# Two interleaved transformer layers on one core: small prices in the planner, and TensorE's order written anew

## The chip, the cores and the metric

The kernel runs on one core of a Trainium2 chip. The metric is the device time of one execution in microseconds (us); smaller is better. Below, TensorE is PE in the profile (its weight loads are PEld), VectorE is DVE, ScalarE is ACT, GpSimd is POOL, and SyncE, which issues most DMAs, is SP.

## The reference

Two layers of the same kind follow each other, with the same weights. Each is an attention over short segments that hands a small memory on from one segment to the next, and then a gated feed-forward network:

```python
for s in range(n_seg):                       # 64 segments of 32 rows
    h = concat([mem, xs])                    # 8 memory rows + 32 rows, 576 wide
    q, k, v = h @ Wq, h @ Wk, h @ Wv         # 32 heads of 128
    p = softmax(where(mask, q @ k.T * scale, -1e9))
    o = (p @ v) @ Wo
    mem = o[:, :M, :]                        # the next segment needs it
    outs.append(o[:, M:, :])
...
x = x + A(layernorm(x)); x = x + B(layernorm(x))   # B: (silu(x w1) * (x w3)) w2, 576 -> 4608 -> 576
x = x + A(layernorm(x)); x = x + B(layernorm(x))
```

The memory makes the segments of a layer a chain: segment s+1 can't start before segment s has its output.

## The kernel before

Both layers run at once, the second eight segments behind the first (`LAG`). There are 72 steps: in steps 0 to 7 the first layer alone is in work, in steps 8 to 63 both are, side by side in the columns of one operand (80 columns in place of 40), and in steps 64 to 71 the second alone. The feed-forward work of groups of four segments is filled in between.

`make_nodes` makes a list of some thousand pieces of work (`Node`), each with an engine, a price in us, the pieces that it depends on, and the buffers that it takes and frees (eight PSUM banks among them). Of TensorE's pieces, every kind has a letter (`KINDS`): `Q`/`q` the projections to queries and keys (576 = 4 x 128 + 64 contraction rows; the lower-case letter is the 64-row rest), `S` the scores of eight heads, `T` a transposition of the probabilities by matmul (in the steps with one layer; with two a DMA transposes them), `P` probabilities by values, `O`/`o` the output projection, `X x V v G g` the values, `F`/`f` the feed-forward's first matmuls, `W`/`w` its second, and `m a b p n` transpositions of rows.

The order of TensorE's pieces is written out as a string of letters, `ORDER = FIRST + FOUR * 11 + LAST`. FIRST has 773 letters, FOUR 208 (four steps; it is played eleven times), LAST 664. `plan` walks through the string and gives the pieces of the other engines, and the DMAs that SP issues, their places by playing the prices through: whichever engine has a piece that can start earliest takes it next. Pieces marked "AD" go to ACT or DVE, whichever comes first. So the string alone sets TensorE's order, and string and prices together set the order on DVE, ACT and on SP's queue, which issues in that order and waits where the next DMA is not yet allowed.

TensorE can use its array whole (`full`: 128 rows by 128 columns) or in parts that work side by side: `row` is two halves of 64 rows, `col` two halves of 64 columns, `c32`, `oct` and `quad` smaller parts of the value projections. Some pieces can run in one shape alone (`q` and `f` in row, `o` and the two-layer `S` in col, `Q` and `O` in full). Others can run in full or col ("full/col": `F`, `P`, `W`, `w`, `T`, `G` and the transpositions): in col every matmul of 128 output rows is issued as two of 64 (`mm`, lines 619 to 627). `plan` decides it by runs: a run of neighbours that can share a shape has that shape, and full where a run leaves the choice open. So a flexible piece next to an `o` or an `S` becomes col and saves a change of shape. A change is priced at `SWITCH = 0.098`.

All matmuls are recorded on line 627, all ACT work on line 630, DVE on 633, SP's loads on 636, the transposing DMAs on 1050. A transposing DMA (`ptd`) needs the probabilities from DVE, and `P` needs it landed. The weights of the feed-forward come in pieces by SP as their two buffers (`w13`) come free, which is when `F` and `f` of the piece two before are done.

At the very start, the first `Q` of step 0's units 0 and 4 (a unit is four heads) is preceded by 12 matmuls on the identity ("W,ident"), three on each quarter of the key weights as it lands; `qk` issues them only where the unit's `Q` comes ahead of its `q` (the name `first`).

Of the kernel before, what the change touches and what calls it, by code (L numbers as in the profile page):

```python
# [54 lines left out]

class Node:
    __slots__ = ("eng", "dur", "fn", "deps", "prio", "mode", "acq", "rel", "name", "lat", "outs", "left", "ready",
                 "start", "end", "by")

    def __init__(self, eng, dur, fn, deps=(), prio=0.0, mode=None, acq=(), rel=(), name="", lat=None):  # L60
# [3 lines left out]
        self.lat = lat  # L64
# [15 lines left out]
def plan(nodes, pools, letters):  # L80
# [119 lines left out]
def ewh(*ns):  # L200
# [2 lines left out]


FIRST = (
    "amQqQqqQqSTQQQqSqqqQSQSTXxVvPPTTOoPPOOooOoQQqqqqQSQQSqvVqQqqTSQPQOSToXPTOPTOPoxoOoQQqqqqQSQvVQSqqQqqQQSSTTPPOaOT"
    "oTPoPOOooQQqqqVvSQQqqQSQQqQqSTqPSxTXOPoTTOPPoOOooQqqpQQSQqqvVSnQqfFqqQQTSFqfTPQFOSfToPWOPfFTOPFOooofWQQqqqqQSQQS"
    "FFffqvVqqqQQQWTTSSFPffxXFPWOoTOPTFPOOoooffFQWQqqqqQQSFSfqVvfFQQqqWSQQFfqfTFSTPWPTOOoPofFTOPFOooWQqqfQQSQqqVvSFfQ"
    "qQqaWqqTQTPSQObSPoXXTTxxPOPOOoooQpqqqQQqSQvqnQfSFVfFqQQqfSFQPWqfSPFFOfOoPWoOofPFOoFfqqQQQQqqWSFSfqqQQqgqGSQQFPfg"
    "GWSfFPOGgfgFGoPOOPWOoooFFqfqfQQWSqqQQvFSqfVQQqqWSQFqfQfPaSFPOoOPoWOffFPFOooWQQqqqqQSQQbQqqSGSqgqQQPgGSOoPGggGPOO"  # L210
    "PooOoQqqqppQQQSvqqVnnQQSFqffFQQSqqfFSwPWPOOFffFooPwPOWOFooFqqffQQWQQwqqfFSFSqfqQwQQWGSqgqQFPfSGgggGPGOPoOOPwOWoo"
    "oFFqfqfQQQQqqfSWFVvwSFFqffqQQQQSqqWwPFSffPOOooFPwOWPFOooafQQqqWqSqqQQQQSqwbSQgqqQGSggGPGPOGPgoOPOOooo"
)
# [4 lines left out]
LAST = (  # L218
    "QqqqppQQQvSqVnSnqqQQQFSfqqQPFOSPofFOPwWOFPfooOofQQqqWwSFfqfFQQQQqfqqFWwGSSFffgqQFPGQWgqwOSoPFggfGGPOFPOOoooWwfqQ"
    "QQQvqqqVSSFqffQFQQQqqqwSWSPFPfOFOwWoPffFPOOoooWQQqqFSwfqfFQQqqWSQQQqqqQSVSbvVPwOPxvXoPOOPooOoQqqvppQVqqQSQQqqnnQ"  # L220
    "SFfqfqQQTSFSPTFPwOWTffoFPTOPOOoooWwFfqqfQQFSQvVqqqQQSQTWFqfqqQQSwSTPFffFOPwWoFTTffFPOPOOoowoXxvQQqqVqqQSQWSFqqfq"
    "QQQTSwqfQPFTSTOPWOFffoPTFOPWOooowVvfqqFQQQqqfSwQWSFFfqqqQQTWTSQPqPQOSwbOTXPxooTOPoOoQqqqpQQSQVqvQSqqQqnSQqTfQfPT"
    "SFPOOTFPooTOPwOfooFVvfqqQQFqqQSQFSwQqqfQQTSfqqFPQOTSXwPToxfOPTFPOOoooFfqqQQqqQSQQFSQfqqvVSwQQqqFTTSPPfFTOOfoPoTw"
    "POOooFfvVqqqQQwSQqQqfqQSFQQqqfSQTSTPPOOFToTPfPOOooopwfFFnFwffFFwffFFwwffFfFwFffFwFfFwffFFwffFfFwFfFwffFw"
)
ORDER = FIRST + FOUR * 11 + LAST

# [8 lines left out]
def make_nodes(em, nseg, pools, o=Opt, dma_bw=230e3, load_bw=400e3):  # L236
# [4 lines left out]
    def node(*a, **k):  # L241
        n = Node(*a, **k)
        nodes.append(n)
        return n
# [90 lines left out]
    def vg_nodes(t, g, deps, tail_deps):  # L335

        b = banks()
        for s in b:
            s.users = 2
        m_ = node("PE", 8 * 0.2158, em.vg(t, g, b, False), deps=deps, prio=t + o.vm, mode="full/col", acq=b, name="VG")  # L340
# [21 lines left out]
    def step(t):  # L362
# [18 lines left out]
        for g in range(NG):  # L381
            qs, qe = [], []
            for u in (2 * g, 2 * g + 1):
                q = Slot("qkt", users=1)
                b = banks()
                pq = t + o.qk + o.ustep * u
                m_ = node("PE", 32 * mm80, em.qk(t, u, b), deps=hx + hm[:1] + ([ld_h[u // 4]] if t == 0 else []),
                          prio=pq, mode="full", acq=[q] + b, name="QK")
                n = node("PE", 4 * mm80, em.qk_tail(t, u, b), deps=hx + hm + ([ld_h[u // 4]] if t == 0 else []), prio=pq + o.qkt, mode="row",
                         acq=[q] + b, name="QKt")  # L390
                rd += [m_, n]
                me[f"QK{u}"], me[f"QKt{u}"] = m_, n
# [22 lines left out]
                pts_of[t, g] = pe_[0]  # L415
            else:
                bt = banks(nl)
                tr = node("PE", 8 * (0.0258 if nl == 1 else 0.0358), em.ptr(t, g, pb, bt), deps=[pbs], prio=pf + o.tr, mode="full/col", acq=[pts] + bt, rel=[pb], name="TR", lat=0.265)
# [6 lines left out]
            b = banks()  # L425
            ot = Slot("ot")
            pv = node("PE", 8 * mm80, em.pv(t, g, pts, b), deps=pe_ + vx_ev["VM", t, g] + vx_ev["VX", t - e, g],
                      prio=pf + o.pv, mode="full/col", acq=b + [ot], rel=[pts], name="PV")
# [4 lines left out]
            wo = node("PE", 32 * mm80, em.wo(t, g, ot), deps=ote + ([ld_o[g]] if t == 0 else []), prio=t + o.wo + o.wog * g, mode="full",  # L433
                      acq=[y] if g == 0 else [], name="WO")
            wot = node("PE", 4 * mm80, em.wo_tail(t, g, ot), deps=[wo], prio=t + o.wo + o.wog * g, mode="col", rel=[ot], name="WOt")
            if g:
# [33 lines left out]
    def job(j):  # L470
# [36 lines left out]
        for at, pp in enumerate([npp - 1] + list(range(npp - 1)) if last else range(split, npp)):  # L507
# [5 lines left out]
            for pr_ in (2 * pp, 2 * pp + 1):  # L513
# [8 lines left out]
                else:  # L522
# [7 lines left out]
                htt = Slot("htt", users=ne)  # L530
                rel13 = [w13] if w13 else []
                fm = node("PE", 16 * mm, em.ffn_up(ents, pr_, w13, b, last and not stays, False), deps=wr + ld, prio=prio, mode="full/col",
                          acq=b + [htt], rel=rel13, name="FF")
# [7 lines left out]
            for (bi, g) in ents:  # L541
                b = banks()
                d = node("PE", 8 * 0.1225, em.ffn_down(em.col(bi, g), pp, htts, w2s, b, last and not stays), deps=mids + lds, prio=prio + o.w2,
                         mode="full/col", acq=b, rel=htts + w2s, name="W2b" if bi else "W2")
                if last and at == npp - 1:
                    xn = Slot("xn")
                    for h in (0, 1):
# [845 lines left out]
```

## Time and profile before

| what | us |
|---|---|
| three runs | 2629.52, 2633.95, 2636.86 (median 2633.95) |
| the profiled execution, whole | 2636.17 |
| its span in the profile | 2634.4 |
| PE busy in the span | 2575.8 |
| DVE busy, ACT busy | 2005.6, 1271.2 |
| FIRST ends, LAST begins (from the span's start) | 523.30, 2202.05 |

The page's lines and groups name an instruction by what it writes and reads ("bank<-HT,W" is a matmul into a PSUM bank with operands HT and W), its active rows and columns of the array ("128*64" is a half-column matmul), the output's size, and how often it came. In the timeline the columns are the start, the length until the last end, the instruction and its count; overlapping rows are normal, since matmuls are pipelined. The time that a piece takes on TensorE is therefore read from its first start to the next piece's first start.

### The profile page before, as it was taken

What the parts mean: (1) busy time and instruction counts of PE and PEld (TensorE: products, weight loads), DVE (VectorE), ACT (ScalarE), POOL (GpSimd) and SP (SyncE); (2) the same over time, 40 slices, a digit from 0 to 9 for tenths busy, and PEclk for the clock granted to TensorE, in tenths of its full rate; (3) what the DMA queues carried; (4) which work ended last, traced back from release to release, by engine and by line L of the source; (5) the groups of instructions that cost most, each with busy time, mean ns of one, the idle gap of its engine ahead of it and who ended that gap; (6) DMA issues with size and microseconds to landing.
All of it is one profiled execution on the core that took longest, in us unless ns stands there. A gap on an engine that the chain in (4) does not pass through costs nothing.

```text
span 2634.4 us, 133901 instructions
## 1 busy us (share of the span) xinstructions
PE 2575.8 (98%) x59670; PEld 2222.5 (84%) x59670; DVE 2005.6 (76%) x5125; ACT 1271.2 (48%) x3757; POOL 197.5 (7%) x253
## 2 busy tenths in 40 slices
PE   6999999999999999999999999999999999999998
PEld 4787888889888888988888888888888888888886
DVE  4787776887778678777867877787777778787876
ACT  2655553444545454444545444454545445454552
POOL 1100000000000000000001000000100101010000
PEclk8999999999999999999999999999999999999999
DMA  9065746565554656556555655655465563545357
GB/s 324 4 187 122 190 104 150 128 153 134 126 145 113 144 128 155 132 131 146 112 142 124 158 140 126 148 116 139 115 159 144 132 155 99 141 120 147 103 165 241
DMA packets 683202, 371.50 MB, mean 141 GB/s; under 512 B 233752, under 2 KB 672800, under 8 KB 681984
## 3 DMA queue, kind: packets, MB, share of 16 engines
q1 hardware_dynamic: 678944, 355.00, 53.4%
q8 instruction: 466, 7.63, 1.2%
q0 software_dynamic: 3024, 6.93, 0.9%
q10 hardware_dynamic: 656, 1.02, 0.2%
q14 instruction: 112, 0.92, 0.1%
HBM read 306.72 MB, written 2.36 MB: 117 GB/s over the span
## 4 chain that ended last, share of the span: by engine, by line
PE 93%; DMA 3%; DVE 3%; ACT 1%; issue 1%; SPq 0%; ACTq 0%; DVEq 0%
PE bank L627 93%; DMA PTS<-PB 2%; DVE HTT L633 1%; DVE STAT L633 1%; DVE SME L633 0%; DVE PB L633 0%; DMA XN<-in_A_x_dram 0%; DVE V L633 0%; DMA W<-in_A_Wk_dram 0%; DMA W<-in_B_w_dram 0%; ACT V L630 0%; ACT HT L630 0%; ACT QKT L630 0%; DVE XR L633 0%; ACT HTT L630 0%
## 5 line engine op out<-in xcount | busy, mean ns | idle before, releaser
L627 PEld LDWEIGHTS <-W 128*128 128x128 bf16 (+2 forms) x32728 | 1260.4, 101 | 106.4 <-issue 59.0
L627 PE MATMUL bank<-HT,W 128*128 128x80 bf16 (+3 forms) x23040 | 788.1, 197 | 12.6 <-ACT HT L630 6.7
L627 PE MATMUL bank<-XTB,W 128*64 128x256 bf16 (+5 forms) x9688 | 657.1, 264 | 1.8 <-DMA W<-in_B_w_dram 0.9
L630 ACT ACTIVATE QKT<-bank 128x192 bf16<-128x192 f32 (+4 forms) x1680 | 381.9, 311 | 264.8 <-PE bank L627 260.6
L627 PE MATMUL bank<-OT,WO 128*128 128x80 bf16 (+3 forms) x11520 | 412.3, 198 | 1.3 <-issue 0.6
L627 PEld LDWEIGHTS <-WO 128*128 128x128 bf16 (+1 forms) x11520 | 382.1, 102 | 27.6 <-issue 15.2
L630 ACT ACTIVATE V<-bank 32x512 bf16<-32x512 f32 (+1 forms) x577 | 327.5, 585 | 132.3 <-PE bank L627 124.0
L627 PE MATMUL bank<-WV,HT 128*32 128x512 bf16 (+4 forms) x3480 | 362.7, 383 | 0.8 <-issue 0.8
L627 PE MATMUL bank<-W2C,HTT 128*64 128x288 bf16 (+1 forms) x3488 | 322.6, 287 | 0.0
L630 ACT ACTIVATE HTT<-bank 128x512 bf16<-128x512 f32 (+1 forms) x322 | 173.6, 555 | 274.7 <-PE bank L627 272.3
L633 DVE TENSOR_REDUCE STAT<-SME 104x8 f32<-104x320 f32 (+1 forms) x576 | 273.7, 475 | 17.8 <-ACT SME L630 11.3
L633 DVE TENSOR_TENSOR PB<-SME,STAT 40x128 bf16<-40x128 f32 (+4 forms) x912 | 274.7, 335 | 8.9 <-DVE STAT L633 0.4
L630 ACT ACTIVATE OT<-bank 128x320 bf16<-128x320 f32 (+1 forms) x408 | 153.0, 407 | 251.9 <-PE bank L627 216.0
L627 PEld LDWEIGHTS <-HT 128*32 128x32 bf16 (+4 forms) x3480 | 144.0, 98 | 149.7 <-issue 33.7
L633 DVE SCALAR_TENSOR_TENSOR HTT<-HTT,bank 128x512 bf16<-128x512 bf16 (+1 forms) x322 | 201.5, 626 | 90.2 <-ACT HTT L630 88.5
L633 DVE SCALAR_TENSOR_TENSOR XR<-bank,XR 128x288 f32<-128x288 f32 x574 | 240.9, 447 | 27.8 <-PE bank L627 24.6
L627 PEld LDWEIGHTS <-HTT 128*64 128x64 bf16 (+1 forms) x3560 | 233.9, 107 | 32.0 <-DVE HTT L633 4.1
L1047 POOL MEMSET PB<- 128x1024 bf16 x142 | 134.7, 951 | 1634.0 <-DMA PTS<-PB 1057.2
L630 ACT ACTIVATE SME<-SME 104x320 f32<-104x320 f32 (+1 forms) x288 | 135.2, 469 | 206.3 <-DVE SME L633 204.4
L633 DVE CAST V<-bank 64x512 bf16<-64x512 f32 (+1 forms) x287 | 196.8, 686 | 42.6 <-PE bank L627 35.9
L633 DVE TENSOR_TENSOR HTT<-HTT,bank 128x512 bf16<-128x512 bf16 (+1 forms) x322 | 203.3, 631 | 30.1 <-PE bank L627 1.4
L633 DVE TENSOR_TENSOR SME<-bank,maskb 104x320 f32<-104x320 f32 (+1 forms) x288 | 139.3, 484 | 57.9 <-PE bank L627 53.3
(59 smaller groups left out, 1383.6 us busy)
## 6 DMA issues: line engine op xcount, KB each, us to landing
W<-in_B_w_dram SPq DMA_DIRECT2D x608, 256.0 KB, 3.5
W2C<-in_B_w_dram SPq DMA_DIRECT2D x304, 288.0 KB, 3.4
W<-in_B_w_dram SPq DMA_DIRECT2D x608, 32.0 KB, 3.6
W<-in_B_w_dram SPq DMA_DIRECT2D x8, 1024.0 KB, 10.9
W<-in_A_Wq_dram SPq DMA_DIRECT2D x9, 512.0 KB, 9.5
WO<-in_A_Wo_dram SPq DMA_DIRECT2D x4, 1152.0 KB, 16.8
XR<-in_A_x_dram POOLq DMA_DIRECT2D x16, 288.0 KB, 2.9
WV<-in_B_w_dram SPq DMA_DIRECT2D x4, 1152.0 KB, 7.2
```

The costliest lines, as they stand in the source:

```text
L627: self.ch("PE", self.nc.tensor.matmul(out, lhsT=lhsT, rhs=rhs, start=start, stop=stop, skip_group_check=True, **k))
L630: self.ch("ACT", self.nc.scalar.activation(*a, **k))
L633: self.ch("DVE", getattr(self.nc.vector, fn_)(*a, **k))
L1047: return lambda n: self.ch("POOL", self.nc.gpsimd.memset(self.pbt(pb), 0.0))
```

## The change

`Node` gets a price `wide`. In `plan`, the prices `wide` of a run add up (`owed`), and are added to the length once the run has turned out to be col. So a flexible piece has one price in full and a slightly higher one in col. Six kinds get such a price, and the projections of a step with one layer, and the 64-row rests, get 8 to 20 ns more. Nothing in how a piece is computed changes; but all three strings are new. All strings keep their lengths and the letters in them.

```diff
@@ plan @@
-    mode, run = [], []
+    mode, run, owed = [], [], 0.0
...
                 dur += SWITCH
                 settle()
-                mode = n.mode
+                mode, owed = n.mode, 0.0
             mode = [m for m in mode if m in n.mode]
+            owed += n.wide
+            if mode == ["col"]:
+                dur += owed
+                owed = 0.0
             run.append(n)
@@ make_nodes: new arguments @@
 VG   + wide=0.005
 QK     32 * mm80 -> 32 * mm80 + (0.02 if nl == 1 else 0.0)
 QKt    4 * mm80  -> 4 * mm80 + (0.014 if nl == 1 else 0.008)
 TR   + wide=0.04
 PV   + wide=0.014 if nl == 2 else 0.045
 WO     32 * mm80 -> 32 * mm80 + (0.016 if nl == 1 else 0.0)
 FF   + wide=0.01
 W2   + wide=0.005
@@ the start of FIRST @@
-    "amQqQqqQqSTQQQqSqqqQSQSTXxVvPPTTOoPPOOoo
+    "maqqqQQSQqQQQSqQqqqQSTSTxXvVPPOTTOoPoPOo
...
@@ FOUR @@
-    "QqqqppQVSvQQnnQfqqFSFqfqQQQfqSFSwPWPOFoffOFPWwOPFOoooFqqffQQQQqqWSwGSFfqgqQQWPQQSwFffqqFGSgggGPGPOOowOPWOoooFFqq"
-    "ffQQQQSWVvfqqFSQQqqwPFSFqqffQQwOSWPoFFPffOOwPWOoooFfqqQQqqaSQQqqWSQQqqQQSbwSggGGPGPOoggGPOPOOooo"
+    "QqqqppQVSvQnQnQFfqqFSfqQQQqfqSFSWPwPOFoffFOPWwOPFOoooFqffqQQQQgqqwSWGSFqfqQQQPWQSwFqqffFSGgggGPGPOwOooOPWOFooFqf"
+    "fqQQQSVvqfqQQFQWqqSwPFSFqfqfQQwOSWoPFFffPOOWPwOoooFqfqQQqqaSQQWqqSQqqQQQSbwSggGGPGPOoggGPOPOOooo"
```

What the program then holds: 58,082 matmuls, before 59,670. Of the 1,588 fewer, 1,576 come of flexible pieces that are now full where they were col (each such matmul is one instead of two): 54 of the 322 `F`, 50 of the 288 `W` and `w`, 28 of the 288 `P` (22 with two layers, 6 with one) and 11 of the 64 `T`. The other 12 are the identity matmuls of unit 0, since its `q` now comes ahead of its `Q`. In one FOUR, 3 `F`, 3 `W`/`w` and 1 `P` go from col to full. Changes of shape along TensorE's order: 1,234, before 1,249; leaving col 311 (326), leaving full 417 (413), leaving row 402 (405), leaving one of the small parts 104 (105).

More of the change, by code (lines that the diff above doesn't have):

```diff
@@ L57, with __init__ @@
     __slots__ = ("eng", "dur", "fn", "deps", "prio", "mode", "acq", "rel", "name", "lat", "outs", "left", "ready",
-                 "start", "end", "by")
-    def __init__(self, eng, dur, fn, deps=(), prio=0.0, mode=None, acq=(), rel=(), name="", lat=None):
+                 "start", "end", "by", "wide")
+    def __init__(self, eng, dur, fn, deps=(), prio=0.0, mode=None, acq=(), rel=(), name="", lat=None, wide=0.0):
         self.eng, self.dur, self.fn, self.prio, self.mode = eng, dur, fn, prio, mode.split("/") if mode else mode
@@ new lines @@
+    "fqQQQSVvqqqQQQSFqqfqQQwWSSfPFPOFOWwoffPFPOOooowQQqqqFSWffFQQqqWSQqqqQQQvSSVVbPwPOOvXooPxPOOooQQppvqqVqqQSQQqnnQS"
+    "FqfqTQQqfSFTSPFWPwTOoffFPTOPOOwoooWVvqfqFQQFfqQSQFqqqfQWwSQQSFqqffFQTwPTSWPOTFoffPTOOPFOxoooXVvqqQQWwSFfqqqQQQSQ"
+    "fqqqFQSQTWwSPFTOPToffFTPwPOOOoooWVvqfqQQFSQfqqQwWFSFfqqqQQTWSPQTQPqOOSobTXPwTOPoxoOoQQqqpQSqqQVvSQnqQqQSFqqfTTQf"
+    "PPSFOToOPFwTOPFOoooffVvqqqQQQSQqfqqQSQFTqqQSPQwTOSPFFTffXxoOPTwPOOoooFQQqqqfQQqSSQQFvqqfVSqwQQFqTTSfPFfPOToOwPTF"
+    "POOooofVvqqqQQwQSQqqqfQSFQQSqqQTSTPPOFOfToToPfPOOoopwfFFnFwffFFwffFfFwwfFfFwFffFwFffFwFffFwFffFwFfFwffFw"
@@ L339, in vg_nodes @@
             s.users = 2
-        m_ = node("PE", 8 * 0.2158, em.vg(t, g, b, False), deps=deps, prio=t + o.vm, mode="full/col", acq=b, name="VG")
+        m_ = node("PE", 8 * 0.2158, em.vg(t, g, b, False), deps=deps, prio=t + o.vm, mode="full/col", acq=b, name="VG", wide=0.005)
         n = node("PE", 0.2158, em.vg(t, g, b, True), deps=deps + tail_deps, prio=t + o.vm, mode="row", acq=b, name="VGt")
@@ L386, in step @@
                 pq = t + o.qk + o.ustep * u
-                m_ = node("PE", 32 * mm80, em.qk(t, u, b), deps=hx + hm[:1] + ([ld_h[u // 4]] if t == 0 else []),
+                m_ = node("PE", 32 * mm80 + (0.02 if nl == 1 else 0.0), em.qk(t, u, b), deps=hx + hm[:1] + ([ld_h[u // 4]] if t == 0 else []),
                           prio=pq, mode="full", acq=[q] + b, name="QK")
-                n = node("PE", 4 * mm80, em.qk_tail(t, u, b), deps=hx + hm + ([ld_h[u // 4]] if t == 0 else []), prio=pq + o.qkt, mode="row",
+                n = node("PE", 4 * mm80 + (0.014 if nl == 1 else 0.008), em.qk_tail(t, u, b), deps=hx + hm + ([ld_h[u // 4]] if t == 0 else []), prio=pq + o.qkt, mode="row",
                          acq=[q] + b, name="QKt")
@@ L417, in step @@
                 bt = banks(nl)
-                tr = node("PE", 8 * (0.0258 if nl == 1 else 0.0358), em.ptr(t, g, pb, bt), deps=[pbs], prio=pf + o.tr, mode="full/col", acq=[pts] + bt, rel=[pb], name="TR", lat=0.265)
+                tr = node("PE", 8 * (0.0258 if nl == 1 else 0.0358), em.ptr(t, g, pb, bt), deps=[pbs], prio=pf + o.tr, mode="full/col", acq=[pts] + bt, rel=[pb], name="TR", lat=0.265, wide=0.04)
                 pe_ = [node("AD", ew(320), em.pt_ev(t, g, i, b, pts), deps=[tr], prio=pf, rel=[b], name="PTe") for i, b in enumerate(bt)]
@@ L427, in step @@
             pv = node("PE", 8 * mm80, em.pv(t, g, pts, b), deps=pe_ + vx_ev["VM", t, g] + vx_ev["VX", t - e, g],
-                      prio=pf + o.pv, mode="full/col", acq=b + [ot], rel=[pts], name="PV")
+                      prio=pf + o.pv, mode="full/col", acq=b + [ot], rel=[pts], name="PV", wide=0.014 if nl == 2 else 0.045)
             pvs[t, g] = pv
@@ L432, in step @@
             ote = [node("AD", ew(4 * c80), em.ot_ev(t, g, ab, b[ab], ot), deps=[pv], prio=pf, rel=[b[ab]], name="OTe") for ab in (0, 1)]
-            wo = node("PE", 32 * mm80, em.wo(t, g, ot), deps=ote + ([ld_o[g]] if t == 0 else []), prio=t + o.wo + o.wog * g, mode="full",
+            wo = node("PE", 32 * mm80 + (0.016 if nl == 1 else 0.0), em.wo(t, g, ot), deps=ote + ([ld_o[g]] if t == 0 else []), prio=t + o.wo + o.wog * g, mode="full",
                       acq=[y] if g == 0 else [], name="WO")
@@ L543, in job @@
                 d = node("PE", 8 * 0.1225, em.ffn_down(em.col(bi, g), pp, htts, w2s, b, last and not stays), deps=mids + lds, prio=prio + o.w2,
-                         mode="full/col", acq=b, rel=htts + w2s, name="W2b" if bi else "W2")
+                         mode="full/col", acq=b, rel=htts + w2s, name="W2b" if bi else "W2", wide=0.005)
                 if last and at == npp - 1:
```

25 lines of the change are left out of this document (10 added, 15 removed).

## The prediction

> **What bounds the kernel.** First the page: the engines' busy times and the chain of work that ended last.
>
> ```profile
> PE 2575.8 (98%) x59670; PEld 2222.5 (84%) x59670; DVE 2005.6 (76%) x5125; ACT 1271.2 (48%) x3757; POOL 197.5 (7%) x253
> ...
> PE 93%; DMA 3%; DVE 3%; ACT 1%; issue 1%; SPq 0%; ACTq 0%; DVEq 0%
> ```
>
> TensorE is busy for 2575.8 of 2634.4 us and carries 93% of the chain. So two things can change the time: how long TensorE takes for its own work, and the 58.6 us in which it stands idle. The view of busy times by stretches says where these lie (columns: the stretch, its length, then busy time and count for PE, PEld, DVE, ACT, POOL, the granted clock, the DMA share and GB/s). The third border, 523.30, is where FIRST ends, the fourth, 2202.05, where LAST begins.
>
> ```profile
> 0.00:12.48 12.48, 0.00 (x1) 0.01 (x1) 8.19 (x16) 0.00 (x0) 5.69 (x17) 1.00 0.86 220
> 12.48:42.56 30.08, 21.40 (x402) 14.09 (x402) 9.48 (x29) 6.89 (x19) 0.00 (x0) 0.88 1.03 408
> 42.56:523.30 480.74, 463.81 (x11925) 393.72 (x11923) 364.88 (x984) 247.20 (x727) 39.19 (x48) 0.99 0.53 134
> 523.30:2202.05 1678.75, 1673.11 (x37312) 1459.16 (x37312) 1293.57 (x3256) 818.37 (x2454) 124.55 (x154) 1.00 0.57 136
> 2202.05:2634.40 432.35, 417.46 (x10034) 355.50 (x10033) 329.49 (x842) 198.70 (x559) 28.05 (x34) 0.99 0.52 149
> ```
>
> Length less PE busy: 12.5 us before the first matmul, 8.7 until 42.56, 16.9 in the rest of FIRST, 5.6 in all eleven FOURs together, 14.9 in LAST. The FOURs are 64% of the span and have almost no idle time, so there only the work itself can shrink. The idle time that an order could save lies in FIRST and LAST, 31.8 us.
>
> **The change, part by part.** The prices are of the plan; what the chip gets is a new order and, by it, other shapes. Their cost is read from the timeline of TensorE, from a piece's first start to the next one's.
>
> ```profile
> 1908.08 1.94 PE L627 MATMUL bank<-XTB,W 128*64 128x256 bf16 x32
> 1909.85 0.37 PE L627 MATMUL bank<-QKT 128*64 128x40 bf16 x15
> ...
> 1919.88 0.48 PE L627 MATMUL bank<-PTS,V 128*64 128x80 bf16 x16
> 1920.16 1.18 PE L627 MATMUL bank<-W2C,HTT 128*64 128x288 bf16 x16
> 1921.14 0.48 PE L627 MATMUL bank<-PTS,V 128*64 128x80 bf16 x16
> 1921.56 1.32 PE L627 MATMUL bank<-OT,WO 128*128 128x80 bf16 x32
> 1922.71 1.91 PE L627 MATMUL bank<-XTB,W 128*128 128x256 bf16 x16
> 1924.55 0.33 PE L627 MATMUL bank<-OT,WO 128*64 128x80 bf16 x8
> ...
> 1928.27 0.45 PE L627 MATMUL bank<-PTS,V 128*128 128x80 bf16 x8
> 1928.55 2.13 PE L627 MATMUL bank<-W2C,HTT 128*128 128x288 bf16 x16
> 1930.51 1.31 PE L627 MATMUL bank<-OT,WO 128*128 128x80 bf16 x32
> ...
> 1931.94 1.91 PE L627 MATMUL bank<-XTB,W 128*128 128x256 bf16 x16
> 1933.69 1.86 PE L627 MATMUL bank<-OT,WO 128*128 128x80 bf16 x56
> ```
>
> *Changes of shape.* A full `F` followed by a full piece takes 1.75 us (1931.94 to 1933.69), one followed by a col piece 1.84 (1922.71 to 1924.55): leaving full costs 0.09. `P` in col takes 0.28 before another col piece (1919.88 to 1920.16) and 0.42 before a full one (1921.14 to 1921.56): leaving col costs 0.14. With 15 fewer exits from col, 4 more from full, and 4 fewer from row and the small parts, which I price like full, that is -15 x 0.14 + 0 = -2.1 us. At 0.09 for every exit it would be -1.4; I take -2.0, nearer to the col row.
>
> *Col turned into full.* With two layers nothing is gained beside the exits: `F` takes 1.77 in col (1908.08 to 1909.85) and 1.75 in full, `P` 0.28 and 0.28 (1928.27 to 1928.55), `W` 0.98 (1920.16 to 1921.14) and 0.98 (half of 1928.55 to 1930.51). With one layer the pieces are short and the doubled count shows:
>
> ```profile
> 51.95 0.55 PE L627 MATMUL bank<-ident,PB 104*128 104x40 bf16 x16
> 52.35 1.55 PE L627 MATMUL bank<-OT,WO 128*128 128x40 bf16 x40
> ...
> 2528.33 0.41 PE L627 MATMUL bank<-PTS,V 128*64 128x40 bf16 x16
> 2528.58 0.41 PE L627 MATMUL bank<-ident,PB 104*64 104x40 bf16 x16
> 2528.83 0.28 PE L627 MATMUL bank<-OT,WO 128*64 128x40 bf16 x8
> ```
>
> `T` takes 0.20 in full (two from 51.95 to 52.35) and 0.25 in col (2528.58 to 2528.83), the one-layer `P` 0.25 in col; I take 0.20 for it in full, as for `T` with the same count and width. So 11 `T` and 6 `P` save 17 x 0.05 = 0.85 us. The 54 `F` at 0.02 would add 1.1, at the most; at the least nothing. I take -0.9, bounds -2.0 and -0.8.
>
> Here the Trainium skill (TensorEngine Tiling (Array Packing), Restrictions and Gotchas) speaks for more: column tiling excludes fast weight load. By that, full pieces should load weights faster, and the 1,576 that turn full should gain beyond the exits; the equal 1.75 and 1.77 above say that the loads are covered. It has a rival of its own below.
>
> *The start.* The identity matmuls of unit 0 go, and `T` no longer follows directly on the first `S`.
>
> ```profile
> 17.35 4.87 PE L627 MATMUL bank<-W,ident 128*128 128x512 bf16 x12 [3.94 <-DMA W<-in_A_Wk_dram]
> 22.44 4.59 SPq L636 DMA_DIRECT2D WV<-in_A_Wv_dram  x4
> 29.33 0.45 PE L627 MATMUL bank<-ident,PB 104*128 104x40 bf16 x8 [3.51 <-DVE PB L633]
> 42.56 5.72 PE L627 MATMUL bank<-WV,HT 64*32 64x512 bf16 x80
> ...
> WV<-in_A_Wv_dram SPq DMA_DIRECT2D x4, 1024.0 KB, 14.7
> ```
>
> Both are covered by loads: the 4.87 us of identity matmuls lie where the key weights' quarters arrive, and the 3.51 us wait of `T` ends long before the value weights are there, whose last load is issued at about 26.7 (22.44 + 4.59, less one issue of 0.3) and lands some 14.7 later, at 41.4. The value projections begin at 42.56, so at most 1.2 us is to be had at their start. I take -1.0. Bounds: 0 if the loads move with it, -4.9 if the identity matmuls were in the way after all.
>
> *The steady FOURs.* An undisturbed FOUR (the first row below) takes 152.20 us, 0.34 of it idle: the first `Q` needs the memory rows of the last `O`, with nothing between. Both strings end in "OOooo" and begin with "Q", so this stays. What is late next is a transposing DMA. In a FOUR's first step SP issues it behind feed-forward loads:
>
> ```profile
> 1745.04:1897.24 152.20, 151.86 (x3392) 132.60 (x3392) 117.56 (x296) 74.42 (x224) 11.32 (x14) 1.00 0.55 136
> ...
> 1757.41 4.50 SPq L636 DMA_DIRECT2D W<-in_B_w_dram  x8
> 1757.65 0.37 PE L627 MATMUL bank<-QKT 128*64 128x40 bf16 x15
> 1762.02 3.78 SPq L1050 DMA_TRANSPOSE PTS<-PB  x2
> 1768.82 0.52 PE L627 MATMUL bank<-PTS,V 128*64 128x80 bf16 x16
> ...
> L1050 SPq DMA_TRANSPOSE PTS<-PB x224: 1222/1244/2422, 242.8 to 2346.7; - x112
> ...
> DMA to landing us min/median/max: 2.6/3.3/6.0
> ```
>
> An issue takes 1.24, so the second of the two starts at about 1764.56 (1762.02 + 3.78 - 1.24), lands 3.3 later at 1767.9, and its `P` starts at 1768.82: 0.9 us of slack. The new string has "FfqqFSfq" where the old one had "fqqFSFqf": the second `S`, at 1757.65 above, comes behind one more `F`, 1.75 us later, while its `P` keeps its place in the string (the 36th letter). On SP's queue the first transposition now stands between the loads of two pairs, ahead of the second half of the eight issues (2.25 of 4.50 us), and the second one behind that half, as before. Who waits behind it is one `P`, and behind that `P` all of TensorE. From that `S` to the issue it took 6.9 us, while the softmax alone, with nothing in its way, held the first `T` up for the 3.51 us quoted above. So some 3 us of the 6.9 are waits for DVE and SP that need not grow. I take 0; bounds 0 and 11 x (1.75 - 0.9) = +9.4 us. Elsewhere in FOUR the work between an `S` and its `P` is the same, longer, or shorter by less than its slack.
>
> *Waits in FIRST and LAST.* I counted the places where the string leaves too little work, by such start-to-start times, between a piece and what it needs: `T` under 4.6 us after its `S`, `P` under 0.6 after its `T`, `O` under 0.8 after its `P`. Before there are 15, 11 and 14 of them, after 12, 6 and 16: 34 for 40, in an idle time of 31.8 us that has other causes too (late DMAs, the last group's feed-forward). Six of 40 places by half of 31.8 is -2.4 us. I take -2.0; bounds -10 (a third of it goes) and +6 (two new late DMAs of the longest one's size, 2.78):
>
> ```profile
> 262.99 0.48 PE L627 MATMUL bank<-PTS,V 128*64 128x80 bf16 x16 [2.78 <-DMA PTS<-PB]
> ```
>
> **Sum:** -2.0 - 0.9 - 1.0 + 0 - 2.0 = -5.9 us. The profiled execution took 2636.2, so 2630.3 in its like; it stands 2.2 over the median of the three runs, 2633.95, from which the forecast is **2628 us**. Its own range, by the bounds of the small terms, is 2622 to 2634.
>
> **Rivals.** What a measurement can tell from no change is about 0.3% here, 7.9 us: faster is below 2626, slower above 2642.
>
> A, *the waits of FIRST and LAST go too.* The third of 31.8 us that its bound has, in place of 2.0, gives 2634 - 3.9 - 10 = 2620. For it: these strings were the least regular, and 11 one-layer `T` and 6 `P` there lose a col neighbour. Against it: the longest waits are for DMAs and the chain of the last group, which no order of these letters shortens.
>
> B, *slower: the second transposition of each FOUR's first step is late.* It decides from the point at which the softmax's end moves by more than 0.9 us when its `S` moves by 1.75. At the full 1.75 it costs 9.4: 2628 + 9.4 = 2637. With landings 0.5 us later for the closer issues behind the loads it is 2643. For it: DVE is 76% busy, so little can be caught up. Against it: 3 us of the chain are waits.
>
> C, *the change does nothing:* the exits are hidden in other waits, only the pieces' counts change: 2634, between 2631 and 2637.
>
> D, *the weight loads are exposed:*
>
> ```profile
> L627 PEld LDWEIGHTS <-W 128*128 128x128 bf16 x20336 | 783.3, 99 | 52.2 <-issue 29.3
> ...
> L627 PEld LDWEIGHTS <-W 128*64 128x64 bf16 x6496 | 336.1, 110 | 3.5 <-issue 0.9 <-DMA XN<-in_A_x_dram 0.2 <-DMA W<-in_B_w_dram 0.2
> ```
>
> Two half loads of 110 ns in place of one of 99: 1,576 x (220 - 99) ns = 191 us less loading, of which a tenth on the path would give 2634 - 19 = 2615. This is what the rule of the Trainium skill (TensorEngine Tiling (Array Packing), Restrictions and Gotchas) would make of it. The equal lengths of `F` speak against it.
>
> **How the numbers follow.** The forecast's case has 0.48, A 0.22, B 0.16, C 0.11, D 0.03. Faster by over 0.3%: A, D, and a quarter of the forecast's case (0.12): 0.37. Slower by over 0.3%: the later part of B and what I haven't seen: 0.11. Within 0.3%: 0.52. The range for 8 in 10 is 2618 to 2639: it holds A's 2620 and B's 2637, and leaves out D, the worst of B and the best of A.
>
> **What would show it.** FOURs of the new kernel should start about 0.15 to 0.2 us closer than the 152.20 quoted; if they take more, look for PE waiting for "DMA PTS<-PB" at the `P` of the first step (B). If FIRST ends by 520 and LAST takes 429, the terms of the waits are right; much earlier is A. PEld's busy time should fall by some 190 us with TensorE's busy time falling by 3 or so; by much more would be D. Two FOURs with equal idle time but a longer busy time would make the exits' price wrong.

## The result, and the profile after

| | before | after |
|---|---|---|
| median, 8 runs each on one chip | 2632.14 | 2641.12 |
| lowest and highest | 2627.84, 2638.15 | 2635.06, 2646.06 |
| ratio | | 1.0028, 95% interval 1.0019 to 1.0037 |
| again, on another chip (23 and 8 runs) | 2633.55 | 2638.66, ratio 1.0016 (1.0005 to 1.0027) |
| the profiled execution, its span | 2636.17, 2634.4 | 2640.42, 2638.1 |

The changed kernel is slower, by 9.0 us in the first comparison and 5.1 in the second. The forecast was 5.9 us faster, and its range ended at 2639. Of the changed kernel, the page's busy times (name, us, share, count) and the shares of the chain:

```profile
PE 2565.3 (97%) x58040; PEld 2205.8 (84%) x58082; DVE 2006.9 (76%) x5088; ACT 1270.5 (48%) x3794; POOL 196.1 (7%) x253
...
PE 88%; DMA 5%; DVE 4%; SPq 1%; issue 1%; ACT 1%; ACTq 0%; DVEq 0%
```

TensorE is busy for 10.5 us less than in the profile of before (2575.8), and the span is 3.7 longer. Most of the 10.5 is not real: 42 matmul records are missing here (58,040 for 58,082 loads), and in a second profile of before (e8 below), where some are missing too, the sum is 2566.8. Against that profile the changed kernel's busy time is only 1.5 us less. On the chain, 5 points have gone from PE to DMA, DVE and SP's queue: a little work was saved, and more than that was lost in waits. The view by stretches says where, first of the changed kernel and then of that second profile of the kernel before. The borders are each kernel's own: the end of step 0, of step 3, of FIRST, of the FOURs. A step is said to end here where its last `O` starts. FIRST and the FOURs end with the weight load of the next `Q`, 0.41 us before its first matmul, which was the border in the prediction's view (522.89 for 523.30 there).

```profile
42.56:62.98 20.42, 14.49 (x273) 9.20 (x273) 11.15 (x27) 8.29 (x18) 2.51 (x3) 0.58 0.95 314
62.98:128.18 65.20, 60.20 (x1950) 50.95 (x1947) 48.88 (x135) 39.72 (x114) 6.21 (x7) 0.97 0.02 4
128.18:524.45 396.27, 389.13 (x9361) 331.70 (x9364) 310.23 (x818) 199.46 (x605) 30.58 (x38) 1.00 0.60 146
524.45:2206.28 1681.83, 1666.75 (x36403) 1448.72 (x36433) 1293.59 (x3245) 817.35 (x2464) 123.08 (x154) 1.00 0.55 135
2206.28:2638.13 431.85, 416.61 (x9692) 351.93 (x9690) 327.34 (x826) 199.38 (x576) 28.07 (x34) 0.99 0.53 149
```

```profile
42.56:56.60 14.04, 11.13 (x266) 7.53 (x259) 9.56 (x21) 7.08 (x16) 2.51 (x3) 0.79 1.10 376
56.60:120.30 63.70, 59.86 (x1967) 50.43 (x1966) 47.63 (x138) 39.40 (x110) 6.16 (x7) 1.00 0.07 20
120.30:517.24 396.94, 389.81 (x9694) 333.77 (x9697) 307.29 (x824) 200.27 (x600) 30.64 (x38) 1.00 0.59 146
517.24:2197.84 1680.60, 1667.48 (x37283) 1458.89 (x37313) 1294.36 (x3256) 818.30 (x2453) 124.73 (x154) 1.00 0.57 135
2197.84:2630.04 432.20, 417.20 (x10036) 355.67 (x10034) 329.64 (x842) 198.86 (x560) 28.09 (x34) 0.99 0.52 149
```

The first row stands out: the rest of step 0 takes 20.42 us for 14.04, and the granted clock over it is 0.58 for 0.79. Steps 1 to 3 take 1.5 more, the FOURs 1.2 more, LAST the same. A single stage has to be read with care, since four profiles of the kernel before differ: FIRST ends at 522.89, 517.24, 518.23 and 520.57, and the FOURs take 1678.75, 1680.60, 1680.38 and 1681.99. Step 0 differs by 1.4 among them.

The timeline of the changed kernel in step 0, PE with the rows of ACT and DVE that take the values out of PSUM; in brackets is the idle time ahead of a row and what ended it:

```profile
43.32 1.05 PE L631 MATMUL bank<-WV,HT 64*32 64x512 bf16 x16
45.65 0.57 ACT L634 ACTIVATE V<-bank 32x512 bf16<-32x512 f32 x1
46.27 0.62 PE L631 MATMUL bank<-WV,HT 128*32 128x512 bf16 x4 [1.89 <-ACT V L634]
47.30 0.67 DVE L637 CAST V<-bank 32x512 bf16<-32x512 f32 x1
48.02 5.73 PE L631 MATMUL bank<-WV,HT 128*32 128x512 bf16 x60 [1.14 <-DVE V L637]
53.15 3.62 ACT L634 ACTIVATE V<-bank 32x512 bf16<-32x512 f32 x6 [6.94 <-PE bank L631]
55.61 0.27 PE L631 MATMUL bank<-PTS,V 128*128 128x40 bf16 x4 [1.86 <-ACT V L634]
```

Before, the 80 matmuls of the value projections were one row (42.56, 5.72 us long). Here the 16 of the 64-row rests run, and then TensorE waits twice, 1.89 and 1.14 us, for one eviction on ACT and one on DVE of values that the other 64 matmuls have not yet added to. The second wait is followed by 60 matmuls in 5.73 us. The granted clock was at 0.50 before the first wait already (from 42.56 on), and it stayed there until near the end of these matmuls (0.59 over 48.02 to 53.75). In e8 it came back sooner: 0.50 over 42 to 44, 0.71 to 46, 1.00 to 48.

The code explains the order (comments added). In step 0 the piece `X` issues no matmuls; it leaves them to `V`, so that both sets share a pass over the weights:

```python
def v_run(self, t, b, strips, tail):
    if t or tail:
        self.v_mm(t, [(b, strips)], tail)
        return
    self.v0.append((b, strips))        # step 0: X only notes its banks
    if len(self.v0) == 2:
        self.v_mm(t, self.v0, False)   # V issues the matmuls of both
```

The plan knows nothing of it: for it, X's banks are complete when `X` and `x` are done, plus 0.205 us. The old string has X, x, V, v there, so `V` starts before that. The new one has x, X, v, V: `v` (0.216 us) lies between, and the first two of X's evictions get a place ahead of `V`, which then has to wait for them since it writes the same banks. By this, two of the eight pieces of the first segment's values are taken out with the sum over the 64-row rest alone, in the changed kernel and in each kernel below that has its FIRST unaltered (e4, e10), e9 apart. These two pieces lack the other 512 of 576 rows, so they are wrong, and "nothing in how a piece is computed changes" does not hold for them.

### The profile page after: what moved, and what is told of

The parts are those of the page before. It is cut to its first block, busy times and chain, and to the rows that moved or that the text cites. A ratio compares the mean times of both kernels' runs of the same rounds, so it can differ in the third digit from the quotient of the medians.

```text
span 2638.1 us, 130711 instructions
## 1 busy us (share of the span) xinstructions
PE 2565.3 (97%) x58040; PEld 2205.8 (84%) x58082; DVE 2006.9 (76%) x5088; ACT 1270.5 (48%) x3794; POOL 196.1 (7%) x253
## 4 chain that ended last, share of the span: by engine, by line
PE 88%; DMA 5%; DVE 4%; SPq 1%; issue 1%; ACT 1%; ACTq 0%; DVEq 0%
PE bank L631 88%; DMA PTS<-PB 3%; SPq L640 1%; DVE HTT L637 1%; DVE STAT L637 1%; DMA W<-in_A_Wk_dram 1%; DVE PB L637 1%; DVE SME L637 1%; DMA W<-in_B_w_dram 1%; DMA XN<-in_A_x_dram 0%; DVE V L637 0%; DVE XR L637 0%; ACT HT L634 0%; ACT HTT L634 0%; DMA W2C<-in_B_w_dram 0%
## 5 line engine op out<-in xcount | busy, mean ns | idle before, releaser
L631 PE MATMUL bank<-HT,W 128*128 128x80 bf16 (+3 forms) x23040 | 802.2, 197 | 19.6 <-ACT HT L634 8.6
L634 ACT ACTIVATE QKT<-bank 128x64 bf16<-128x64 f32 (+4 forms) x1727 | 394.8, 311 | 303.5 <-PE bank L631 294.1
L634 ACT ACTIVATE V<-bank 64x512 bf16<-64x512 f32 (+1 forms) x565 | 319.3, 585 | 135.3 <-PE bank L631 127.6
L631 PE MATMUL bank<-WV,HT 128*32 128x512 bf16 (+4 forms) x3439 | 357.2, 385 | 9.4 <-issue 6.0
L637 DVE CAST V<-bank 64x512 bf16<-64x512 f32 (+1 forms) x299 | 205.1, 686 | 51.9 <-PE bank L631 46.1
```

Source lines behind the costliest of these rows:

```text
L631: self.ch("PE", self.nc.tensor.matmul(out, lhsT=lhsT, rhs=rhs, start=start, stop=stop, skip_group_check=True, **k))
L634: self.ch("ACT", self.nc.scalar.activation(*a, **k))
L637: self.ch("DVE", getattr(self.nc.vector, fn_)(*a, **k))
```

## The experiments

Lengths are from one profile each; "ratio" is to the kernel before on the same chip.

| kernel | median (runs) | ratio, 95% | step 0 ends | step 3 ends | FIRST | FOURs | LAST |
|---|---|---|---|---|---|---|---|
| before, first profile | 2632.14 (8) | | 57.0 | 121.7 | 522.89 | 1678.75 | 432.76 |
| e8 before | 2631.68 (8) | 0.9995 (0.9985 to 1.0005) | 56.6 | 120.3 | 517.24 | 1680.60 | 432.21 |
| e15 before | 2633.61 (1) | | 55.6 | 120.6 | 518.23 | 1680.38 | 433.23 |
| e16 before | 2637.85 (1) | | 56.3 | 120.7 | 520.57 | 1681.99 | 433.51 |
| after | 2641.12 (8) | 1.0028 (1.0019 to 1.0037) | 63.0 | 128.2 | 524.45 | 1681.83 | 431.86 |
| e10 after | 2638.66 (8) | 1.0016 (1.0005 to 1.0027) | 62.9 | 128.3 | 520.25 | 1682.03 | 432.38 |
| e1 X, x, V, v | 2636.32 (12) | 1.0013 (1.0005 to 1.0022) | 57.4 | 124.4 | 518.81 | 1681.14 | 431.75 |
| e18 the same | 2638.89 (11) | 1.0015 (1.0006 to 1.0024) | 58.1 | 124.6 | 521.44 | 1681.66 | 434.99 |
| e9 evictions behind V | 2636.77 (12) | 1.0011 (1.0002 to 1.0021) | 57.9 | 124.4 | 519.65 | 1680.77 | 434.04 |
| e7 e1, identity back | 2636.88 (11) | 1.0013 (1.0004 to 1.0022) | 57.1 | 122.1 | 517.81 | 1679.08 | 435.19 |
| e13 old step 0 | 2636.06 (9) | 1.0015 (1.0004 to 1.0026) | 57.0 | 122.8 | 517.58 | 1682.61 | 434.45 |
| e14 old steps 1 to 3 | 2637.50 (11) | 1.0023 (1.0015 to 1.0032) | 58.2 | 124.5 | 521.95 | 1680.40 | 432.78 |
| e12 old steps 0 to 3 | 2633.83 (11) | 1.0001 (0.9992 to 1.0011) | 55.6 | 122.1 | 520.35 | 1682.39 | 433.89 |
| e17 the same | 2634.87 (11) | 1.0003 (0.9994 to 1.0012) | 55.7 | 122.5 | 516.41 | 1682.46 | 430.96 |
| e3 old FIRST | 2637.98 (7) | 1.0024 (1.0014 to 1.0035) | 55.5 | 121.7 | 521.41 | 1681.94 | 432.66 |
| e4 old FOUR | 2645.73 (6) | 1.0048 (1.0034 to 1.0062) | 60.0 | 125.5 | 520.84 | 1685.16 | 432.49 |
| e11 e1, old LAST | 2650.64 (4) | 1.0061 (1.0042 to 1.0080) | 58.6 | 125.2 | 518.10 | 1684.80 | 447.77 |
| e2 all strings old | 2658.57 (4) | 1.0100 (1.0086 to 1.0114) | 56.3 | 122.5 | 521.03 | 1692.67 | 443.71 |
| e5 e1, old prices | 2643.34 (5) | 1.0043 (1.0030 to 1.0056) | 58.8 | 127.2 | 525.66 | 1680.20 | 434.37 |
| e6 before, new FOUR | 2634.57 (11) | 1.0014 (1.0005 to 1.0023) | 56.9 | 121.8 | 517.80 | 1679.72 | 434.68 |

### Step 0's evictions: e1, e9, e10

e1, the changed kernel with the old order at one place (the 25th to 28th letter of FIRST):

```diff
-xXvV
+XxVv
```

> The changed kernel with two neighbouring letters of step 0 swapped back (v and V), nothing else. In the changed order two of the eight pieces of step 0's first values are taken out of their banks after the 64-row rest only (so those two blocks of the first segment's values lack the other 512 rows), and the main matmuls then wait for them (idle 1.89 and 1.14 us, after which the array runs at half clock). Theory S (the time is lost at the start): step 0 ends about 6 us earlier, the whole time is 5 to 6 us below the changed kernel's 2641.1, about 2635.5. Theory J (late transposing DMAs in the eleven FOURs carry the loss): under 1 us changes, 2640 to 2641.

The edit exchanges both pairs, x with X and v with V, where the expectation names one. Step 0 ends 5.6 us earlier (57.4 for 63.0), and the ratio falls from 1.0028 to 1.0013. e1 exchanges letters, so it could be the order itself that matters. e9 leaves all letters as the changed kernel has them and only tells the plan what `V` does:

```diff
             last_v[:] = v_nodes("VM", t, k, t + o.vm + 0.01 * k, ...
+            for g in range(NG if t == 0 else 0):
+                for ev in vx_ev["VX", 0, g]:
+                    ev.after(last_v[0])
```

> The changed kernel with its strings and prices untouched; in the plan the value evictions of step 0's X banks wait for V as well, so that every piece of the first segment's values is taken out after all of its matmuls. Theory (the two evictions placed ahead of V cost the start some 6 us, the order of the letters itself nothing): FIRST within 2 us of the 518.8 us of the kernel with the letters exchanged, last O of step 0 at about 57 us and not 63, median 2636.5 within 2. Rival (the order x, X, v, V is itself worse, or the rest of FIRST had been fitted to the late start): FIRST stays at 523 or more and the median at 2639 to 2642.

```profile
42.01 5.82 PE L634 MATMUL bank<-WV,HT 64*32 64x512 bf16 x80
47.24 4.22 ACT L637 ACTIVATE V<-bank 32x512 bf16<-32x512 f32 x7 [2.74 <-PE bank L634]
50.29 0.27 PE L634 MATMUL bank<-PTS,V 128*128 128x40 bf16 x4 [2.46 <-ACT V L637]
```

The same timeline of e9: the 80 matmuls are one row again, 5.82 us long, where the changed kernel took from 43.32 to 53.75. All evictions come behind them. FIRST (519.65), step 0 (57.9) and the median (2636.77) came out as the theory said. e10 is the changed kernel a second time, on e9's chip:

> The changed kernel once more, for a second profile. Both theories: the same median as before (2641.1 within 2), the last O of step 0 at 63 us again. What it tells apart: if the waits for transposing DMAs in the FOURs are chance, their sum over eleven FOURs moves by 1 to 3 us against the first profile and sits at other cycles and other letters; if the new order sets them, they sit at the same letters of the string.

Its median was 2638.66, under the expected 2639.1, so the two changed-kernel comparisons differ by more than I had thought; step 0 again ended at 62.9, with the same waits of 1.89 and 1.14 us. So the early evictions cost 5 to 6 us at the end of step 0, seen in both profiles. At the end, 1.9 us of it are left between e10 and e9 on one chip, where the two intervals overlap, and 5.7 between the first result (+9.0) and e1 (+3.3) on two. How much of step 0's loss reaches the end is therefore not settled.

### The identity matmuls: e7

```diff
 FIRST, start (of e1)
-maqqqQQS
+maQqqqQS
```

> The changed kernel with v and V swapped back and, at the start, the first Q ahead of the three q, so that the 12 identity matmuls of unit 0 are issued again. If they are covered by the key weights' landings, as the prediction had it, nothing changes: 2635 to 2637.5. If they warm the array's clock for what follows, some 1 to 3 us are won; if they stood in the way, up to 5 are lost.

2636.88 for e1's 2636.32, on another chip, ratios equal: no cost or gain of the 12 matmuls shows, as the prediction had it, though the intervals would hide one of 2 us.

### What else the first steps lose: e3, e12, e13, e14, e17, e18

With the evictions mended, 3 to 5 us remain, in three kernels (1.0011, 1.0013, 1.0013). In steps 1 to 3 the new string leaves a little less between an `S` and its `T` (112 letters in all between the twelve pairs, for 121; no `T` stands directly behind its own `S`, as two expectations have it). TensorE's waits for the softmax's probabilities there (us in total, times, longest), in the changed kernel, then before (e8), then with the old letters (e17):

```profile
PE bank L631 <- DVE PB L637: 3.0, 5, 1.2
```

```profile
PE bank L627 <- DVE PB L633: 0.8, 2, 0.4
```

```profile
PE bank L631 <- DVE PB L637: 1.3, 2, 0.9
```

e3 put back all of FIRST, e12 its first 161 letters (steps 0 to 3), e13 the first 42 (step 0), e14 the 43rd to 161st (steps 1 to 3, with X, x, V, v):

```diff
 e12  FIRST = old FIRST[:161] + new FIRST[161:]
 e13  FIRST = old FIRST[:42] + new FIRST[42:]
 e14  FIRST = e1 FIRST[:42] + old FIRST[42:161] + new FIRST[161:]
```

> The changed kernel with the old FIRST (new prices, new FOUR and LAST). Theory S: the 6 us of the start are won back, but what the new FIRST saves between steps 5 and 8 (5.5 us in the profiles, from 6.3 late to 0.8 late) is lost again, unless that is a chance wait of the old kernel's profile: 2635 to 2641. Theory J: 2639 to 2642, as FOUR is unchanged.

> The changed kernel, with the letters of steps 0 to 3 (the first 161 of FIRST) as the old string has them and all later letters as the new one has them. Theory (the new letters lose at two places of the start: some 6 us at step 0 and, with the T directly behind its S, some 3 us more in steps 1 to 3; what comes later is worth about nothing): last O of step 3 at 120 to 122 us in place of 124 to 128, waits of TensorE for the softmax's P there at most 1.7 us in place of 3.0, and a median within 2 us of before. Rival (what is lost at the start is caught up by step 16 anyway, and the rest of the difference comes later): last O of step 3 early, but step 16 not, and a median 3 us over before, as for the kernels of which only step 0 was mended.

> The changed kernel with the letters of step 0 alone (the first 42 of FIRST) as the old string has them. Theory 1 (what is left after the evictions are back behind V is in the rest of step 0's order): last O of step 0 at 55.6 us as with the first 161 letters old, and a ratio of 1.000 to before. Theory 2 (it is in steps 1 to 3, where T waits 3.0 us for the softmax): waits for P there 3.0 us again, steps 1 to 3 some 67 us long, and a ratio of 1.0010 as for the two kernels in which only the evictions were put back.

> The changed kernel with the order X, x, V, v at step 0 and the letters of steps 1 to 3 alone (43 to 161 of FIRST) as the old string has them. Theory 1: last O of step 0 at 57.4 us, ratio 1.0010 as without the old letters in steps 1 to 3. Theory 2: waits for the softmax's P in steps 1 to 3 at most 1.7 us, these steps 65 us long or less, and a ratio of 1.000.

e12 is level with the kernel before (1.0001). But neither half alone is: e13 has 1.0015 and e14 1.0023. So theory 1 failed at e13, and theory 2, which e13 fits, failed at e14, where the waits for P fell to 1.3 us and steps 1 to 3 still took 66.3.

The granted clock is part of the answer. Over steps 1 to 3 it was 0.94 in e14. In the six profiles with 1.00 there (the first of before, e8, e16, e6, e7, e4) these steps took 63.8 to 65.5 us, in all others, with 0.94 to 0.98, 64.9 to 68.5. One of these others is e15, the kernel before. In step 0, e12 and e13 have the same letters and end it at 55.6 and 57.0: the 80 matmuls of the values took 4.31 us at a clock of 1.00 in e12, and 5.73 at 0.74 in e13. So such lengths from one profile hold 1 to 3 us that the letters alone don't set.

To see whether e12 was chance, it ran again beside e1's kernel on one chip:

> The kernel with the old letters in steps 0 to 3 again, now on the same chip as the one with only the order X, x, V, v put back. If the old letters of steps 0 to 3 are worth the 3 us, its ratio is 1.000 and 0.001 under the other's; if its first median was chance, both have 1.001 to 1.002.

> The kernel with the order X, x, V, v put back, beside the one before it: ratio 1.0010 to 1.0015, either way.

2634.87 and 2638.89, 4.0 us apart, though their intervals overlap. With e12, the two kernels with the old letters have 1.0001 and 1.0003, the four of e1, e7, e9 and e18 1.0011 to 1.0015: the old letters of steps 0 to 3 together are worth some 2 to 4 us, and the rest of the new strings shows no gain over the old ones. Why it takes both halves is not settled. Step 3 ends at 128.2 in the changed kernel, 124.4 to 124.6 in e1, e9, e14 and e18, 122.1 to 122.8 in e7, e12, e13 and e17, and 120.3 to 121.7 before; but e7 and e13, with 1.0013 and 1.0015, show that an early end of step 3 alone does not bring the time of before. e3, with all of the old FIRST, ended step 3 at 121.7 and had 1.0024. That suggests that the old letters behind step 3 don't fit the new prices; no stage of its profile shows it.

### Strings and prices: e2, e4, e5, e6, e11

```diff
 e2   new prices; FIRST, FOUR, LAST: new -> old
 e4   new prices; FOUR: new -> old
 e5   e1's strings; prices: new -> old
 e6   kernel before; FOUR: old -> new
 e11  e1; LAST: new -> old
```

> The new prices with the old three strings: TensorE's order is that of before, only the order on DVE, ACT and SP may move. If the prices themselves do harm there, the time is above that of before (2632.1) by several us; by theory S and theory J both it is that of before within 2 us, since either sits in the strings.

> The changed kernel with the old FOUR (new prices, new FIRST and LAST). Theory J: the eleven FOURs take 1678.8 us as before in place of 1681.8 and the time falls by 3 us or, if the runs without a profile lose more there, up to 9: 2632 to 2638. Theory S: within 2 us of the changed kernel, 2639 to 2643, and step 0 still ends 6 us later than before.

> New strings with v and V swapped back, but the old prices. TensorE's order is that of the run with the two letters swapped (2636.3); the places on ACT and DVE differ in a few spots of each FOUR, SP's order (A a pair's loads, T a transposition: ATATABB...) does not. Theory Q (the remaining 3 us are waits for DMAs in the FOURs, of SP's new order): 2635.5 to 2637.5, and in the FOURs some 4 us of waits for PTS and W together against 1.1 before. Theory P (the new prices put ACT and DVE in a worse order): 2632 to 2634.

> The kernel before with the new FOUR alone (old prices, old FIRST and LAST). Theory Q: the eleven FOURs take 1681 to 1682 us in place of 1678.8 although their work alone is 1.5 us less, the time is about 2636. Rival (the new FOUR is good, the remaining loss sits in FIRST's and LAST's strings): FOURs 1677 to 1678, time about 2631.5.

> The kernel with the letters of step 0 exchanged, with LAST's string of before. Theory (a string fits only the prices it was searched with, here those of the one-layer steps, which LAST is made of): LAST becomes longer, by about the 11 us that it took with the new prices and all old strings, so 441 to 444 us and a median of 2644 to 2648. Rival (the 11 us came from the state in which the old FOURs left the queues): LAST stays at 432 to 434 us and the median at 2635 to 2638.

The prices alone, under the old strings, cost 25 us (e2), although TensorE's letters are the old ones: 12 in the FOURs and 11 in LAST. e11 lost LAST's part alone, more than expected (447.77 for 441 to 444). e4, with the old FOUR alone, missed both theories: 12.7 us over before, FOURs at 1685.16, waits for the loads (`W`) of 5.5 us in them. e6, the new FOUR under the old prices, came out between its two: FOURs at 1679.72, and 1.0014. e2's waits of TensorE in the FOURs, and the first step of one FOUR on SP and PE:

```profile
PE bank L631 <- DMA W<-in_B_w_dram: 9.9, 14, 1.9
...
688.73 1.22 SPq L1054 DMA_TRANSPOSE PTS<-PB  x1
690.05 5.30 SPq L640 DMA_DIRECT2D W<-in_B_w_dram  x8
...
695.20 0.55 PE L631 MATMUL bank<-XTB,W 64*128 64x256 bf16 x4 [0.45 <-DMA W<-in_B_w_dram]
```

Price changes of 5 to 45 ns moved the first transposition on SP's queue ahead of all eight loads, and the `f` that needs them waits in every FOUR. The changed kernel has the transposition between two fours of loads, as the prediction read from the order:

```profile
688.58 2.12 SPq L640 DMA_DIRECT2D W<-in_B_w_dram  x4
690.87 1.54 SPq L1054 DMA_TRANSPOSE PTS<-PB  x1
692.51 2.28 SPq L640 DMA_DIRECT2D W<-in_B_w_dram  x4
```

One wait carries half of what LAST loses in e2 (5.83 us) and over a third in e11. Here e11's row:

```profile
2610.04 2.35 PE L631 MATMUL bank<-W2C,HTT 128*128 128x288 bf16 x8 [5.54 <-DMA W2C<-in_B_w_dram]
```

The new strings under the old prices (e5) lose in FIRST instead, 525.66, and miss both theories. So a string does best here with its own prices, and "the same letters" is not the same kernel.

### The stages of before: e8, e15, e16

> The kernel before once more, for a second profile of it: how far do its parts vary from run to run? If the wait of 2.78 us for PTS at 262.99 is chance, FIRST ends at 520 here in place of 522.9; FOURs should be 1678 to 1680.

> The kernel before once more, for a third profile. If what is left of the difference (3 us with the evictions mended) sits in the FOURs and LAST, this profile has FOURs of 1679 to 1681 us, waits of TensorE for transposing DMAs and feed-forward loads of 1 to 4 us there, and a LAST of 432 to 433, under the 1681.3 and 433.3 that the eight profiles with the new FOUR and LAST have on average. If it sits in FIRST, the FOURs come out at 1681 or more and FIRST at 517 or less.

> The kernel before, for a fourth profile: the same numbers as for the third are looked for.

With four profiles of before, the FOURs have a mean of 1680.43 and LAST of 432.93. The eleven profiles with the new prices, FOUR and LAST (after, e1, e3, e7, e9, e10, e12, e13, e14, e17, e18) have means of 1681.48 and 433.18. These 1.1 and 0.3 us can't be told from nothing, since single profiles of one kernel differ by 3.2 in the FOURs: e16 alone has 1681.99, and the place could not be told by these two profiles. The wait of 2.78 us for a transposing DMA was not chance: at the same `P` TensorE waited 1.78 us in e8, 1.45 in e15 and 1.70 in e16.

## Why the prediction was wrong

*The start* is the step that failed. The prediction said "at most 1.2 us is to be had at their start. I take -1.0. Bounds: 0 if the loads move with it", so on the slow side nothing was allowed for. It looked only at what comes before the value projections, and took these to be the same 80 matmuls. The exchange of x, X, v, V stood in the diff. What it does to ACT and DVE, whose places string and prices set together, was not worked out. The runs (e9 above all, with all letters kept) put 5 to 6 us in its place at step 0 (63.0 and 62.9, for 57.4 and 57.9 with the evictions behind `V`). Of the 10.4 us from 43.32 to 53.75, 3.03 are the two waits, and the 60 matmuls at 5.73 us are 2.3 more than the 3.4 that 60 take at full clock (an estimate: 40 take 2.25 at 113.12).

This is not the whole miss. With the start mended, 3 to 5 us are lost where 4.9 were to be won. In e12 and e17, which have the old letters in steps 0 to 3 alone, nearly all of the other three terms (-2.0 for the exits, -0.9 for full pieces, -2.0 for waits) should show; their intervals reach down to 0.9992 and 0.9994, that is -2.1 and -1.6 us, and leave no room for -4.9. The second median of the changed kernel, 2638.66, lies inside the range, but by chance: the range's upper part came from B, and B is not what happened.

*The identity matmuls* show no cost either way: right, as far as e7 can tell.

*The steady FOURs.* The shapes came as predicted: an undisturbed FOUR of the changed kernel takes

```profile
2054.21:2206.28 152.07, 151.25 (x3313) 131.70 (x3313) 117.53 (x295) 74.31 (x224) 11.20 (x14) 1.00 0.54 136
```

0.13 less than the 152.20 of before, where 0.15 to 0.2 was expected. Over eleven FOURs that is 1.4 us, yet their sum rose. The waits of TensorE in the FOURs, the changed kernel and then before (e15):

```profile
PE bank L631 <- DMA PTS<-PB: 3.5, 9, 0.7
PE bank L631 <- DMA W<-in_B_w_dram: 2.4, 2, 1.5
```

```profile
PE bank L627 <- DMA PTS<-PB: 3.1, 8, 0.6
...
PE bank L627 <- DMA W<-in_B_w_dram: 0.2, 1, 0.2
```

Together 5.9 us, 5.8 in e10, 3.1 to 6.3 (4.8 on average) in all eleven profiles of the new FOUR and prices; before 3.3, and 1.1, 3.7 and 4.7 in the other three, 3.2 on average. So on average, with much overlap, the saving goes into waits for later DMAs. Rival B had the kind of wait right and the place wrong: its `P` waited once, 0.50 us, at 1925.66. The other waits differ from FOUR to FOUR, but nine of the changed kernel's 11 came again in e10 in the same FOUR and place (seven at the same matmul, among them B's `P` with 0.43 us; two, at an `F` of the third step, eight weight loads later): by e10's test, the new order sets them.

*Waits in FIRST and LAST*, taken at -2.0: LAST was to take 429 and took 431.86 and 432.38, no change. In FIRST the count of places ("34 for 40") summed all places alike, and hid that in steps 1 to 3 the waits for the softmax go from 0.8 to 3.0 us. From step 3's end to the end of FIRST the new letters take 391.9 to 398.3 us (the ten profiles without e3), the old ones 396.9 to 401.2 (four). Some of the loss at the start is made up there; whether by better letters or because late steps wait less for their loads is not separated. The 2.78 us wait that stood behind this term's upper bound comes in all four profiles of before, but its size was taken from the longest one (1.45 to 1.78 in the others). In the changed kernel the longest wait for a transposing DMA in that stretch (195 to 270 us) is 0.7, and e10 has none. So the new order did shorten that wait, which A's "no order of these letters" had excluded.

*D* falls. The loads fell by 1,588 as counted, but PEld's busy time by 16.7 us, not by 190, since overlapping loads count once (the 20,336 loads of 99 ns in the prediction's row are 783.3 us of busy time); and nothing was gained. The Trainium skill (TensorEngine Tiling (Array Packing), Restrictions and Gotchas) has column tiling without fast weight load; in this kernel that shows in no time.

*A* and *C* fall by the result. With the old letters in steps 0 to 3, though, C's "nothing" is what is left of all the rest.

## What to carry to other kernels

Where a written order and a price list together place the work of other engines, read a change of the order on every engine, not only on the one whose letters it holds: four exchanged letters moved two evictions, and 5 to 45 ns of price moved a DMA ahead of eight others. A planner must know which piece really issues an instruction. A step that works for two pieces, priced on one of them, makes the order look legal to the plan, while on the chip it is late, and here wrong in its values. And before the size of a wait goes into a sum, see a second profile: the wait of 2.78 us was there in each of four, but in the other three with 1.45 to 1.78.

## What the runs showed of the hardware

A short idle time of TensorE can cost more than its length. In step 2 of the changed kernel it stood for 1.22 us, and then the granted clock (third number from the end) was at half:

```profile
101.00:102.00 1.00, 0.94 (x37) 0.90 (x34) 0.97 (x3) 0.54 (x4) 0.00 (x0) 1.00 0.00 0
102.00:103.00 1.00, 0.44 (x18) 0.33 (x14) 0.93 (x4) 0.43 (x1) 0.00 (x0) 1.00 0.00 0
103.00:104.00 1.00, 0.34 (x8) 0.26 (x8) 1.00 (x5) 0.00 (x0) 0.00 (x0) 0.97 0.00 0
104.00:105.00 1.00, 0.90 (x16) 0.88 (x16) 0.07 (x1) 0.77 (x2) 0.86 (x1) 0.50 0.00 0
105.00:106.00 1.00, 1.00 (x34) 0.95 (x31) 0.64 (x3) 0.82 (x4) 0.98 (x2) 0.50 0.00 0
106.00:107.00 1.00, 1.00 (x34) 0.96 (x31) 0.33 (x1) 0.32 (x3) 0.00 (x0) 0.50 0.05 16
107.00:108.00 1.00, 1.00 (x42) 1.00 (x38) 0.00 (x0) 0.00 (x0) 0.00 (x0) 0.83 0.00 0
```

That is some 3.4 us at half clock (3 whole microseconds, and a third of the one at 0.83), so 1.7 us of work lost behind 1.22 of waiting. It doesn't come each time. Ten profiles have this wait of 1.22 us (1.21 in one) at the same letters; in eight of them such a stretch at half clock followed, in e4 and e7 none did. Here is e7:

```profile
96.00:97.00 1.00, 0.95 (x35) 0.91 (x32) 0.93 (x4) 0.66 (x3) 0.00 (x0) 1.00 0.00 0
97.00:98.00 1.00, 0.04 (x2) 0.00 (x0) 0.97 (x5) 0.04 (x1) 0.00 (x0) 1.00 0.00 0
98.00:99.00 1.00, 0.63 (x17) 0.54 (x18) 0.68 (x3) 0.27 (x1) 0.26 (x1) 1.00 0.00 0
99.00:100.00 1.00, 1.00 (x42) 0.96 (x37) 0.57 (x3) 0.93 (x4) 1.00 (x2) 1.00 0.07 16
```

The Trainium skill (TensorE: Matmul & The Clock Gate, Why this matters for your kernels) warns of idle gaps over some 3 us; here one of 1.22 was enough in eight of ten profiles. Waits of 0.65 us and less, at 80.51 and 83.58 in the changed kernel, left the clock at 1.00. Yet in e2, e14, e15 and e17 some 3.4 us at half clock followed a wait of 0.47 us in step 2, which in the other three profiles of before left it at 1.00. What decides between the two is not settled by these runs.

In step 0 the two waits of 1.89 and 1.14 us did not start the half clock, which was there before them; but with them it was still at 0.50 over 50 to 52, and in e9, without them, at 0.51 over 42.01 to 45.47 and at 1.00 over 45.47 to 52.30.
